# Retention feeding a multiplicative FFN on one core: the turns of keys and queries move from SyncE to ScalarE

## The chip, the cores and the metric

The kernel runs on one core of one Trainium2 chip. A core has five engines that run their own instruction streams in order: TensorE (PE in the profile, its weight loads PEld), VectorE (DVE), ScalarE (ACT), GpSimd (POOL) and SyncE (SP). They meet only through semaphores. The metric is device time in microseconds of one execution, the median of several. The kernel before takes 191.19 us (three runs, 191.11 to 193.03). One execution of it was profiled.

## The reference, cut to what matters

For four sequences, eight heads, 768 tokens and a head width of 64, a decaying state is built up, token by token, and read by the query. The result, as rows of 512, goes through two projections whose product passes two more matrices:

```
for t in range(S):
    state = gamma * state + einsum('bhd,bhe->bhde', k[:, :, t], v[:, :, t])
    y[:, :, t] = scale * einsum('bhd,bhde->bhe', q[:, :, t], state)
x = y.transpose(0, 2, 1, 3).reshape(B * S, H * D)      # 3072 x 512
out = ((x @ w1) * (x @ w2)) @ w3 @ w_out               # 512 -> 1024 -> 1024 -> 512
```

## The kernel before, in words

The recurrence is cut into chunks of 256 tokens, three to a sequence, twelve in all; the code calls a chunk a **step** and numbers them n = 0 to 11. All engines follow an order written out by hand: the Python order of the calls is the order on each engine, and every wait is put in by the framework from the tiles that are read and written. Each tile has a tag and a number of buffers (`bufs`), and the eight banks of PSUM are given to tags by name (S0, S1, X0, X1, K, F0, F1, F2).

For a step, q, k and v are loaded from HBM as float32 into `st` tiles (fifteen staging buffers; k and v come in two transfers each, q in one), cast to half precision in `q16`, `k16` and `v16` (v is scaled by the decay at the same time), and q and k are turned so that the head dimension lies on the partitions. The first steps turn on TensorE; from step 3 on the turn is a DMA transpose from SBUF to SBUF. The turned tiles feed `scores` (k by q, within the chunk) and `inter` (state by q); the untransposed k and v feed `kv`, whose result updates the state; `mask` and `av` give the chunk's output, `x_out` scales it into `XT`. Then eight units follow, `a_unit` and `b_unit` for u = 0 to 3: each is eight matmuls of 128x128 by 256 columns with w1 or w2. ScalarE copies the result of an a unit to SBUF (`a_evac`, the tile `pa`), and VectorE multiplies it with the result of the b unit (`b_evac`, the tile `ht`). One step later `o_unit` multiplies `ht` with w3 @ w_out, which is made once at the start, ScalarE scales it out of PSUM (`o_copy`, the tile `osb`) and SyncE stores it.

The units of a step share three banks, taken in turn: a0 in F2, b0 in F0, a1 in F1, b1 in F2, a2 in F0, b2 in F1, a3 in F2, b3 in F0. So `b_unit` 2 can start only when `a_evac` 1 has emptied F1, and `b_unit` 3 only when `a_evac` 2 has emptied F0.

The loop at the end of the kernel runs steps 3 to 11. A step from 4 on begins with `inter(n)`, then `ahead(n + 1)` (scores and kv of the next step), `av(n)`, `x_out(n)`, the two `o_unit`s of step n - 1, and the eight units of step n. TensorE runs this in order, so a late operand of `scores(n + 1)` holds everything behind it. SyncE issues every DMA of the kernel: in a step the turn of step n + 2 as one transposing transfer of keys and queries together (16 blocks of 128x128, `turn_pair`, L304), the loads of step n + 4, and the store of step n - 1, which waits for both `o_copy`s (L568). ScalarE casts the queries (`cast_queries`), GpSimd casts the keys and the values (`casts`). Step 3 has its own list, `catch_up`, spread over its units, because the prologue leaves stores and loads behind.

Of the kernel before, what the change touches and what calls it, by code (L numbers as in the profile page):

```python
# [10 lines left out]
HP = mybir.dt.float16  # L11
# [9 lines left out]
def kernel(  # L21
# [11 lines left out]
    nc = tc.nc  # L33
    B, H, S, D = q.shape
    T = 256
# [1 line left out]
    EO = 2  # L37
    NSTAGE = 15
    NS = B * PER
    PAIR = 3 + 2  # L40
    NP = H // 2
    DM = 512
    DFF = 1024
# [6 lines left out]
    att = ctx.enter_context(tc.tile_pool(name="att", bufs=2))  # L50
# [7 lines left out]
    def copy(eng, dst, src):  # L58
        {"v": nc.vector.tensor_copy, "g": nc.gpsimd.tensor_copy, "s": nc.scalar.copy}[eng](dst, src)  # L59

    def tt(eng, dst, a, b, op):
        (nc.vector if eng == "v" else nc.gpsimd).tensor_tensor(dst, a, b, op)  # L62
# [6 lines left out]
    def new_stage():  # L69
        return stage.tile([128, 1024], FP, tag="st", name="st")  # L70
# [4 lines left out]
    def load(nm, n, via=None):  # L75
        via = via or nc.sync
        b, c = divmod(n, PER)
        t = new_stage()
        src = source[nm][b, :, c * T : (c + 1) * T, :]
        if nm == "q" or n < EO:  # L80

            via.dma_start(
                t[:, :].rearrange("p (h x) -> p h x", x=2 * D), src.rearrange("h (p t) d -> p h (t d)", t=2)
            )
        else:
            for s in range(2):
                via.dma_start(  # L87
                    t[:, s * 512 : (s + 1) * 512].rearrange("p (h d) -> p h d", d=D),
                    src[:, s * 128 : (s + 1) * 128, :].rearrange("h i d -> i h d"),
                )  # L90
        tok_in[nm, n] = t
# [14 lines left out]
    w3_st, wo_st, w_st = {}, {}, {}  # L106
# [114 lines left out]


    w3h, w3p, w3t, acc = {}, {}, {}, {}
    w3_free = []

    def cast_wo(i, eng):
        copy(eng, WO[i][:, :, :].rearrange("p a n -> p (a n)"), wo_st[i][:, :])

    def cast_w3(f, eng):
        if not w3_free:  # L230
            pair = att.tile([128, 2, 2, 512], HP, tag="kq16", name="w3h", bufs=3)
            w3_free.extend(pair[:, i, :, :].rearrange("p t c -> p (t c)") for i in range(2))
        w3h[f] = w3_free.pop(0)
        copy(eng, w3h[f], w3_st[f][:, :])

    def turn_w3(f, tag):
        src, ps = w3h.pop(f), bank(tag, [128, 1024], HP)
# [22 lines left out]

    kq16 = {}
    q16, k16, v16, qT, kT, qP, am, XT, TS, KB, X = {}, {}, {}, {}, {}, {}, {}, {}, {}, {}, {}

    def cast(nm, n, eng):
        dst = {"q": q16, "k": k16}[nm]
        if n < PAIR:
            dst[n] = t = att.tile([128, 2, 512], HP, tag=nm + "16", name=nm + "16", bufs=2)
        else:  # L270
            if n not in kq16:
                kq16[n] = att.tile([128, 2, 2, 512], HP, tag="kq16", name="kq16", bufs=3)
            dst[n] = t = kq16[n][:, "kq".index(nm), :, :]
        src = tok_in.pop((nm, n))
        if nm == "q" or n < EO:
            copy(
                eng, t[:, :, :].rearrange("p t (h d) -> p h t d", d=D),
                src[:, :].rearrange("p (h t d) -> p h t d", t=2, d=D),
            )
        else:  # L280
            copy(eng, t[:, :, :].rearrange("p s c -> p (s c)"), src[:, :])

    def cast_v(n, eng):
        v16[n] = t = att.tile([128, 2, 512], HP, tag="v16", name="v16", bufs=3)
        src = tok_in.pop(("v", n))
        if n < EO:
            tt(
                eng, t[:, :, :].rearrange("p t (h d) -> p h t d", d=D),
                src[:, :].rearrange("p (h t d) -> p h t d", t=2, d=D),
                VS[:, :, :].rearrange("p t h -> p h t").unsqueeze(3).broadcast_to((128, H, 2, D)), MULT,  # L290
            )
        else:
            tt(
                eng, t[:, :, :].rearrange("p s (h d) -> p (s h) d", d=D),
                src[:, :].rearrange("p (s d) -> p s d", d=D),
                VN[:, :, :].rearrange("p s h -> p (s h)").unsqueeze(2).broadcast_to((128, 2 * H, D)), MULT,
            )

    def new_T(nm):
        return att.tile([128, 2, NP, 128], HP, tag=nm + "T", name=nm + "T", bufs=2)  # L300

    def turn_pair(n):
        t = att.tile([128, 2, 2, NP, 128], HP, tag="kqT", name="kqT", bufs=2)
        nc.sync.dma_start_transpose(  # L304
            t[:, :, :, :, :].rearrange("p x t a i -> p (x t a) i"),
            kq16[n][:, :, :, :].rearrange("p x t c -> p (x t c)"),
        )
        kT[n], qT[n] = t[:, 0, :, :, :], t[:, 1, :, :, :]

    def dma_turn(nm, n, via=None):  # L310
        src, dst = {"q": (q16, qT), "k": (k16, kT)}[nm]
        dst[n] = t = new_T(nm)
        (via or nc.sync).dma_start_transpose(
            t[:, :, :, :].rearrange("p t a i -> p (t a) i"), src[n][:, :, :].rearrange("p t c -> p (t c)")
        )
# [181 lines left out]
    def two_blocks(W, n, u, tag):  # L497
        ps = bank(tag, [128, 2, T])
        for i in range(2):
            f = 2 * u + i  # L500
            for d in range(4):
                nc.tensor.matmul(  # L502
                    ps[:, i, :], lhsT=W[d][:, f * 128 : (f + 1) * 128], rhs=XT[n][:, d, :],
                    start=(i == 0 and d == 0), stop=(i == 1 and d == 3),
                )
        return ps
# [5 lines left out]
    def b_evac(n, u, ps):  # L512
        if n not in HT:
            HT[n] = fsb.tile([128, 8, T], HP, tag="ht", name="ht", bufs=2)
        tt("v", HT[n][:, 2 * u : 2 * u + 2, :], pa.pop((n, u))[:, :, :], ps[:, :, :], MULT)
# [4 lines left out]
    def b_unit(n, u, tag):  # L520
        b_evac(n, u, two_blocks(W2, n, u, tag))
# [41 lines left out]
    def o_store(n, tb, c0=0, c1=512):  # L563
        r0 = n * T + tb * 128
        nc.sync.dma_start(out[r0 : r0 + 128, c0:c1], o_sb[n][:, tb, c0:c1])  # L565

    def o_store_all(n):
        nc.sync.dma_start(  # L568
            out[n * T : (n + 1) * T, :].rearrange("(t p) c -> p t c", t=2), o_sb[n][:, :, :]
        )  # L570
# [286 lines left out]
    LAST = 3  # L857

    def casts(n):
        if n < NS:  # L860
            cast("k", n, "g")
            cast_v(n, "g")

    def cast_queries(n):
        if n < NS:
            cast("q", n, "s")

    def turns(n):
        if n < NS:
            turn_pair(n)  # L870

    def loads(n):
        if n < NS:
            load("k", n)
            load("q", n, nc.sync)
            load("v", n, nc.sync)

    def catch_up(u):
        if u == 0:
            load("k", LAST + 3)  # L880
            turns(LAST + 2)
            o_store(2, 1)
            o_store(1, 1)
            o_store(2, 0)
            load("q", LAST + 3)
            load("v", LAST + 3)
        elif u == 1:
            load("k", LAST + 4)
        elif u == 3:
            casts(LAST + 3)  # L890

    def ahead(n):
        scores(n, ("S0", "S1"))
        kv(n, ("K", "F1"))

    def ahead_out(n):
        states(n)
        mask(n, 0)
        mask(n, 1)

    LATE = ()
    for n in range(LAST, NS):
        nxt = n + 1 < NS and n > LAST
        late = nxt and n in LATE
        if n > LAST:
            inter(n, ("X0", "X1"))
            fence(n)
            if nxt and not late:
                ahead(n + 1)
            av(n)  # L910
            x_out(n, 0)
            x_out(n, 1)
            if nxt and not late:
                ahead_out(n + 1)
            cast_queries(n + 2)
            turns(n + 2)
            if n == LAST + 1:
                load("q", n + 3)
                load("v", n + 3)
            loads(n + 4)  # L920
            casts(n + 3)
            o_unit(n - 1, 0, ("F2",))
            o_copy(n - 1, 0)
            o_unit(n - 1, 1, ("F0",))
            o_copy(n - 1, 1)
            o_store_all(n - 1)
        tags = ("F2", "F0", "X1" if late else "F1")
        for u in range(4):
            if late and u == 2:
                ahead(n + 1)  # L930
                for i in range(1, 4):
                    state(n + 1, i)
                mask(n + 1, 0)
            a_unit(n, u, tags[2 * u % 3])
            b_unit(n, u, tags[(2 * u + 1) % 3])
            if late and u == 2:
                mask(n + 1, 1)
            if late and u == 2 + 1:
                state(n + 1, 4)
                state(n + 1, 5)  # L940
            if n == LAST:
                catch_up(u)
    cuts = ((0, 320), (320, 512))
    o_unit(NS - 1, 0, ("F2",))
    o_out(NS - 1, 0)
# [32 lines left out]
```

## Time and profile before

| | us |
|---|---|
| median of three runs | 191.19 |
| the profiled execution, its own time | 192.26 |
| span of the profiled execution | 190.6 |
| TensorE busy in the span | 174.9 (92%) |
| ScalarE busy | 71.1 (37%) |
| GpSimd busy | 50.5 (26%) |
| queue of SyncE, its transfers, as a share of 16 DMA engines | 85.6% |

How to read it: the span is what the profiler saw of the program; the own time of the same execution has 1.66 us around it. Busy shares are averages over stages with different limits. A row of a timeline gives the start, the duration, the engine, the line, the operation and the tiles, and in brackets the idle time just before it and what ended it; "SPq" is the queue of SyncE, where the duration of a DMA instruction is the time that SyncE was held by issuing it, not the time of the transfer. Landing times run from the start of the issue until the data has arrived.

### The profile page before, as it was taken

Reading aid. Unit: us, or ns where it says so; the run is one execution under the profiler, and the core shown is the slowest. Engines: PE = TensorE matmul, PEld = TensorE weight load, DVE = VectorE, ACT = ScalarE, POOL = GpSimd, SP = SyncE. Lnnn points to the kernel's source line nnn. Section 1 sums busy time; section 2 is a strip of 40 time slices with the busy share of each in tenths; the row PEclk is TensorE's granted clock in tenths of the full one; section 3 lists DMA queues with packets and bytes.
Section 4 is the critical chain, followed back from the end, with each engine's and each line's share of the span. In section 5 each row is a group of like instructions: output and inputs, shape, how many; then the busy total and the mean of one; then the engine's idle time right before and its main releaser. Section 6 shows DMA issues by size and latency. Waiting matters only on the chain.

```text
span 190.6 us, 5952 instructions
## 1 busy us (share of the span) xinstructions
PE 174.9 (92%) x2592; PEld 125.2 (66%) x2592; DVE 100.6 (53%) x171; ACT 71.1 (37%) x131; POOL 50.5 (26%) x79
## 2 busy tenths in 40 slices
PE   7499998999999884899899969999999999999993
PEld 2254554788757652686785846868868688585872
DVE  2435788526866285538248427474384653744130
ACT  5634434462255202231534333343432432322322
POOL 7852237633230301020505233323033010000000
PEclk9979999999999999699999999999999999999999
DMA  5999999989998998999999999999998270030303
GB/s 218 399 407 357 321 290 381 413 210 235 234 212 185 206 246 179 223 252 241 203 219 193 291 198 243 237 246 229 216 292 215 39 185 3 0 115 0 108 6 110
DMA packets 83402, 40.75 MB, mean 214 GB/s; under 512 B 61232, under 2 KB 77872, under 8 KB 83376
## 3 DMA queue, kind: packets, MB, share of 16 engines
q1 hardware_dynamic: 83376, 40.38, 85.6%
q8 instruction: 20, 0.33, 0.8%
q14 instruction: 6, 0.05, 0.1%
HBM read 29.36 MB, written 6.29 MB: 187 GB/s over the span
## 4 chain that ended last, share of the span: by engine, by line
PE 57%; DMA 22%; SPq 6%; POOL 6%; issue 3%; DVE 2%; ACT 2%; POOLq 0%; DVEq 0%
PE psF L502 29%; PE psF L550 15%; DMA st<-in_k_dram 6%; DMA st<-in_v_dram 5%; DMA st<-in_moe_w_dram 4%; DMA st<-in_q_dram 4%; SPq L87 4%; DMA kqT<-kq 3%; PE psX L443 2%; PE psX L252 2%; PE psS L252 2%; SPq L565 1%; PE psX L468 1%; PE psS L353 1%; POOL v L62 1%
## 5 line engine op out<-in xcount | busy, mean ns | idle before, releaser
L502 PEld LDWEIGHTS <-w 128*128 128x128 f16 x640 | 63.3, 99 | 15.7 <-issue 5.8
L502 PE MATMUL psF<-xt,w 128*128 128x256 f16 x576 | 65.9, 276 | 4.0 <-ACT osb L561 4.0
L62 DVE TENSOR_TENSOR ht<-pa,psF 128x512 f16<-128x512 f32 x39 | 26.8, 687 | 42.3 <-PE psF L502 42.3
L550 PE MATMUL psF<-w3o,ht 128*128 128x512 f16 (+2 forms) x176 | 38.3, 370 | 0.0
L59 ACT COPY pa<-psF 128x512 f32<-128x512 f32 x39 | 22.7, 585 | 41.3 <-PE psF L502 36.6
L550 PEld LDWEIGHTS <-ht 128*128 128x128 f16 x200 | 18.4, 98 | 19.3
L62 POOL TENSOR_TENSOR v<-st,VN 128x1024 f16<-128x1024 f32 x8 | 15.2, 1902 | 33.3 <-DMA st<-in_v_dram 23.6
L561 ACT ACTIVATE osb<-psF 128x512 f32<-128x512 f32 (+2 forms) x22 | 12.6, 576 | 24.3 <-PE psF L550 24.3
L485 DVE TENSOR_TENSOR xt<-psX,YN 128x512 f16<-128x512 f32 x18 | 12.2, 725 | 8.8 <-PE psX L468 8.8
L532 PEld LDWEIGHTS <-w 128*128 128x128 f16 x128 | 12.1, 98 | 2.9 <-ACT w L59 1.3
L62 POOL TENSOR_TENSOR t<-s,GS 128x256 f16<-128x256 f32 x8 | 5.8, 726 | 30.5 <-DVE s L62 30.5
L252 PEld LDWEIGHTS <-w3t 128*128 128x128 f16 x64 | 5.8, 101 | 7.3 <-ACT w3t L59 1.6
L370 DVE TENSOR_TENSOR am<-psS,keep 128x512 f16<-128x512 f32 x15 | 9.6, 681 | 1.2 <-PE psX L353 1.2
L59 ACT CAST kq<-st 128x1024 f16<-128x1024 f32 x7 | 7.3, 1046 | 6.7 <-DMA st<-in_q_dram 6.7
L532 PE MATMUL psF<-xt,w 128*128 128x256 f16 x56 | 9.7, 273 | 0.0
L59 POOL CAST kq<-st 128x1024 f16<-128x1024 f32 x6 | 6.2, 1036 | 12.2 <-DMA st<-in_k_dram 12.2
L443 PEld LDWEIGHTS <-t 64*64 64x64 f16 x320 | 6.2, 109 | 3.1 <-issue 3.0
L240 PEld LDWEIGHTS <-w3h 128*128 128x128 f16 x64 | 4.4, 110 | 4.5 <-DVE w3h L59 3.5
L532 PE MATMUL psX<-xt,w 128*128 128x256 f16 x32 | 6.1, 273 | 0.8 <-ACT w L59 0.8
L502 PE MATMUL psS<-xt,w 128*128 128x256 f16 x48 | 5.7, 272 | 1.0 <-DVE ht L62 1.0
L468 PE MATMUL psX<-am,v 64*64 64x64 f16 (+1 forms) x320 | 6.0, 197 | 0.5 <-ACT fence L456 0.5
L468 PEld LDWEIGHTS <-v 64*64 64x64 f16 x384 | 5.0, 106 | 1.8 <-issue 0.9
(137 smaller groups left out, 201.3 us busy)
## 6 DMA issues: line engine op xcount, KB each, us to landing
st<-in_moe_w_dram SPq DMA_DIRECT2D x16, 512.0 KB, 8.9
st<-in_q_dram SPq DMA_DIRECT2D x12, 512.0 KB, 6.6
st<-in_v_dram SPq DMA_DIRECT2D x20, 256.0 KB, 5.9
st<-in_k_dram SPq DMA_DIRECT2D x20, 256.0 KB, 5.4
out_dram<-osb SPq DMA_DIRECT2D x8, 512.0 KB, 5.0
st<-in_moe_w_out_dram SPq DMA_DIRECT2D x4, 512.0 KB, 7.3
out_dram<-osb SPq DMA_DIRECT2D x7, 256.0 KB, 3.8
st<-in_k_dram SPq DMA_DIRECT2D x2, 512.0 KB, 10.1
```

The source lines that it names most:

```text
L59: {"v": nc.vector.tensor_copy, "g": nc.gpsimd.tensor_copy, "s": nc.scalar.copy}[eng](dst, src)
L62: (nc.vector if eng == "v" else nc.gpsimd).tensor_tensor(dst, a, b, op)
L87: via.dma_start(t[:, s * 512 : (s + 1) * 512].rearrange("p (h d) -> p h d", d=D), src[:, s * 128 : (s + 1) * 128, :].rearrange("h i d -> i ...
L252: nc.tensor.matmul(acc[f][:, :], lhsT=w3t[f][:, g * 128 : (g + 1) * 128], rhs=WO[i][:, r, :], start=(first and r == 0), stop=(last and r = ...
L370: nc.vector.tensor_tensor(t[:, :, :, :].rearrange("p a s i -> p (a s) i"), ps[:, :, :, :].rearrange("p a s i -> p (a s) i"), keep64[:, :]. ...
L443: nc.tensor.matmul(o, lhsT=TS[n, c][half(r), a, :], rhs=rhs, start=((g, r) not in begun), stop=False, skip_group_check=True,)
L468: nc.tensor.matmul(o, lhsT=v16[n][half(g), t, h * D : (h + 1) * D], rhs=rhs, start=((g, r) not in begun), stop=(n >= EO or t == 1), skip_g ...
L485: nc.vector.tensor_tensor(XT[n][:, :, :].rearrange("p a (s x) -> p (a s) x", s=2)[:, :, g * 64 : (g + 1) * 64].rearrange("p k (i t) -> p k ...
L502: nc.tensor.matmul(ps[:, i, :], lhsT=W[d][:, f * 128 : (f + 1) * 128], rhs=XT[n][:, d, :], start=(i == 0 and d == 0), stop=(i == 1 and d = ...
L532: nc.tensor.matmul(rows_ps[w, n, uh][j // 2][:, j % 2, :], lhsT=W[d][:, f * 128 : (f + 1) * 128], rhs=XT[n][:, d, :], start=(first and j % ...
L550: nc.tensor.matmul(ps[:, :], lhsT=HT[n][:, f, tb * 128 : (tb + 1) * 128], rhs=W3O[f][:, c0:c1], start=(f == 0), stop=(f == 7),)
L561: nc.scalar.activation(o_sb[n][:, tb, c0:c1], o_ps.pop((n, tb, c0, c1))[:, :], AF.Copy, scale=final_scale)
```

## The change

The one transposing transfer of a step becomes two of half the size, `kT` and then `qT`, and from step 4 of the loop on (the turns of chunk 6 and later) ScalarE issues them, on a DMA queue of its own: the keys' after the first pair of units of step n, the queries' after the second pair, for step n + 2. The turn of chunk 5 stays with SyncE, also in two transfers. The queries' cast moves from ScalarE to GpSimd, between those of keys and values, one step earlier than before (three steps ahead of use, not two). The loads of a step run three steps ahead, not four. The tiles of casts and turns have three buffers of their own for keys and for queries, and the w3 casts of the prologue have tiles of their own. In step 3 the whole catch-up list stands ahead of the units, with the turn of chunk 5 before the load of chunk 6's keys.

```
     def cast(nm, n, eng):
-        ... (from chunk 5 on k and q share one tile kq16, 3 buffers)
+        dst[n] = t = att.tile([128, 2, 512], HP, tag=nm + "16", name=nm + "16", bufs=3)
...
-    def turn_pair(n):
-        t = att.tile([128, 2, 2, NP, 128], HP, tag="kqT", name="kqT", bufs=2)
-        nc.sync.dma_start_transpose(...)
...
     def casts(n):
         if n < NS:
             cast("k", n, "g")
+            cast("q", n, "g")
             cast_v(n, "g")
-    def cast_queries(n):
-        if n < NS:
-            cast("q", n, "s")
-    def turns(n):
-        if n < NS:
-            turn_pair(n)
+    def turns(n, via=None):
+        if n < NS:
+            dma_turn("k", n, via)
+            dma_turn("q", n, via)
...
-    def catch_up(u):
-        if u == 0:
-            load("k", LAST + 3)
-            turns(LAST + 2)
-            ...
+    def catch_up():
+        turns(LAST + 2)
+        load("k", LAST + 3)
+        o_store(2, 1)
+        o_store(1, 1)
+        o_store(2, 0)
+        load("q", LAST + 3)
+        load("v", LAST + 3)
+        casts(LAST + 3)
...
+    TVIA = (0, 1)
     for n in range(LAST, NS):
...
-            cast_queries(n + 2)
-            turns(n + 2)
-            if n == LAST + 1:
-                load("q", n + 3)
-                load("v", n + 3)
-            loads(n + 4)
+            if not TVIA:
+                turns(n + 2)
+            loads(n + 3)
             casts(n + 3)
...
+        else:
+            catch_up()
...
             a_unit(n, u, tags[2 * u % 3])
             b_unit(n, u, tags[(2 * u + 1) % 3])
+            if TVIA and n > LAST and n + 2 < NS and u in TVIA:
+                dma_turn("kq"[TVIA.index(u)], n + 2, nc.scalar)
```

More of the change, by code (lines that the diff above doesn't have):

```diff
@@ L39 @@
     NS = B * PER
-    PAIR = 3 + 2
     NP = H // 2
@@ L223 @@
     w3h, w3p, w3t, acc = {}, {}, {}, {}
-    w3_free = []
     def cast_wo(i, eng):
@@ L229, in cast_w3 @@
     def cast_w3(f, eng):
[L230 to L234, printed above, removed]
+        w3h[f] = att.tile([128, 1024], HP, tag="w3h", name="w3h", bufs=5)
+        copy(eng, w3h[f][:, :], w3_st[f][:, :])
     def turn_w3(f, tag):
@@ L258, in w3_out @@
         copy(eng, W3O[f][:, :], acc.pop(f)[:, :])
-    kq16 = {}
     q16, k16, v16, qT, kT, qP, am, XT, TS, KB, X = {}, {}, {}, {}, {}, {}, {}, {}, {}, {}, {}
@@ L267, in cast @@
         dst = {"q": q16, "k": k16}[nm]
[L268 to L273, printed above, removed]
+        dst[n] = t = att.tile([128, 2, 512], HP, tag=nm + "16", name=nm + "16", bufs=3)
         src = tok_in.pop((nm, n))
@@ L299, in new_T @@
     def new_T(nm):
-        return att.tile([128, 2, NP, 128], HP, tag=nm + "T", name=nm + "T", bufs=2)
-    def turn_pair(n):
-        t = att.tile([128, 2, 2, NP, 128], HP, tag="kqT", name="kqT", bufs=2)
[L304 to L308, printed above, removed]
+        return att.tile([128, 2, NP, 128], HP, tag=nm + "T", name=nm + "T", bufs=3)
     def dma_turn(nm, n, via=None):
@@ L874, in loads @@
             load("k", n)
-            load("q", n, nc.sync)
-            load("v", n, nc.sync)
-    def catch_up(u):
-        if u == 0:
-            load("k", LAST + 3)
-            turns(LAST + 2)
[L882 to L890, printed above, removed]
+            load("q", n)
+            load("v", n)
+    def catch_up():
[7 more added lines that the diff above has]
+        casts(LAST + 3)
     def ahead(n):
@@ L940 @@
                 state(n + 1, 5)
-            if n == LAST:
-                catch_up(u)
     cuts = ((0, 320), (320, 512))
```

## The prediction

> **What bounds the kernel now.** I read the page first (TensorE busy 92%, no other engine above 53%), then the chain of work that ended last, from step 4 on. In time order, with start and duration in microseconds, its steady part reads:
>
> ```profile
> 117.34 6.99 PE psF L502 x64
> 124.33 0.56 PE psX L443 x28
> 124.95 0.26 PE psS L353 x24
> 125.76 3.56 PE psF L550 x16
> 129.32 6.99 PE psF L502 x64
> ```
>
> This is TensorE alone: eight units (64 matmuls at 0.109, so 0.874 for each half unit), `inter`, `scores`, two `o_unit`s, and 11.98 later the next units. Call the start of a step's units U. Scores begin at U+7.55 (124.89). The first unit copies of ScalarE (92.58, 104.56, 118.26, 130.23 and on to 178.14) lie 11.97 or 11.98 apart, but for one gap of 13.70. The list of what TensorE waited for from 76 on says why:
>
> ```profile
> PE psF L502 <- ACT osb L561: 4.0, 2, 3.3
> PE psS L353 <- DMA kqT<-kq: 1.7, 1, 1.7
> PE psX L468 <- ACT fence L456: 0.3, 1, 0.3
> ```
>
> (total, times, longest). The 3.3 lies before step 3, at the queries' load of step 5. The other wait on `osb` is 0.76, before step 4's units: `o_copy` stood behind the query cast, which waited for its load. The 1.7 is step 6: SyncE, which issues everything one after another, came to the turn of chunk 7 only at 106.55. From there on nothing but TensorE ends last, so anything the change adds shows in full once it outlasts its cover.
>
> **What goes.** At step 4, 0.76: the cast leaves ScalarE. At step 6 the gap of 13.70 is 1.72 over the others; the turn no longer stands behind SyncE's loads, so this goes too. Sum: 2.5 saved. Nothing takes their place from the loads: a step's loads go out right after the previous store, about U+1.2, and land by some U+11; GpSimd casts them from about the next U on (now 1.04 + 1.04 + 1.90, with 0.73 of state, 4.7 of 12), and the turn comes a step after that. Without that step of cover, late loads would cost their lateness once. In the catch-up the queries' load of chunk 6 goes out some 1.3 later (84.71 before, landed 89.9), so the cast ends near 92.3; ScalarE wants it near 94.3. `scores(5)` keeps its turn, issued at 78.35 as before.
>
> **What comes: two turns in ScalarE's stream.** An engine is held while it issues a DMA. The timeline of SyncE has the rows (start, time held), first for 8 blocks, as after the change, then for 16:
>
> ```profile
> 54.78 1.33 SPq L313 DMA_TRANSPOSE kT<-k  x1
> 61.65 4.17 SPq L313 DMA_TRANSPOSE qT<-q  x2
> 67.02 1.29 SPq L313 DMA_TRANSPOSE kT<-k  x1
> ...
> 118.35 3.19 SPq L304 DMA_TRANSPOSE kqT<-kq  x1
> ...
> 150.15 2.93 SPq L304 DMA_TRANSPOSE kqT<-kq  x1
> ```
>
> The two of the second row took 1.34 and 2.72 by the tile's list. So one turn holds its engine for x = 1.29 to 2.72. No row shows ScalarE issuing a DMA; these are its nearest, and I see no reason for less. Into what does x go? ScalarE in the same step:
>
> ```profile
> 118.26 0.58 ACT L59 COPY pa<-psF 128x512 f32<-128x512 f32 x1 [0.28 <-PE psF L502]
> 120.00 0.58 ACT L59 COPY pa<-psF 128x512 f32<-128x512 f32 x1 [1.16 <-PE psF L502]
> 121.75 0.58 ACT L59 COPY pa<-psF 128x512 f32<-128x512 f32 x1 [1.16 <-PE psF L502]
> ```
>
> The gap is 1.16, so every turn overruns it, and the next copy is late. Behind the turn stand `a_evac` 1 and 2, and for them wait the banks of `b_unit` 2 (starts U+4.37) and `b_unit` 3 (U+6.12). With 0.05 between instructions: the keys' turn starts at U+1.55, `a_evac` 1 at 1.60 + x, the queries' turn at 2.23 + x, `a_evac` 2 at 2.28 + 2x, and it ends at 2.86 + 2x. `b_unit` 3 is on time while x stays below some 1.6; `b_unit` 2 below 2.2.
>
> The second clock is the landing. The queries' turn starts at 2.23 + x and must have landed by U+7.55, since `scores(n + 2)` stands in the next step's head and TensorE is in order. From issue to landing (min, median, max) the trace has for `kT` and then `qT`:
>
> ```profile
> DMA to landing us min/median/max: 4.2/4.7/5.2
> ...
> DMA to landing us min/median/max: 3.8/4.9/5.9
> ```
>
> Before, the turn had nearly a whole step. Now, per step:
> - x = 1.31 (the two `kT` rows): the turn starts at 3.54; landing 3.8 gives 7.34, no stall; 4.9 gives 8.44, 0.9 late; 5.9 gives 1.9.
> - x = 2.03 (mean of the `qT` rows): `a_evac` 2 ends at 6.92, `b_unit` 3 is 0.85 late; landing 4.26 + 4.9 = 9.16 against 7.55 + 0.85, another 0.76. Sum 1.6.
> - x = 2.72, landing 5.9: 0.6 at `b_unit` 2, 1.65 at `b_unit` 3, 1.05 at scores. Sum 3.3.
>
> How often? Six steps issue turns, 4 to 9. Loads end with chunk 11's, sent in step 7. The windows by step show the DMA share at 1.02 to 1.09 up to 141, then 0.75 and 0.20; after, a step still has the same transfers (SyncE took 11.4 from one turn to the next, 118.35 to 129.71), and they start at U+1.2, just where the turns are. So steps 4 to 7 run beside loads. In 8 and 9 the last row above is the model: held 2.93 for 16 blocks, landed in 4.6, so 1.47 for 8 blocks and 1.47 + 1.67 = 3.1: the queries land at U+6.9, no stall.
>
> For the loaded steps I take 1.2, between 0.9 and 1.6: both rows are of 8 blocks beside loads. Four times 1.2 is 4.8, less 2.5 is **+2.3**.
>
> **A rule against the row.** The SyncE rows are of one issuer; the loads beside a turn held SyncE 1.05 and 1.07 each (median, keys and values). The Trainium skill, Perfetto Trace Analysis, section "DMA Instruction — HWDGE (DVE, Sync)", says that the descriptor generator is shared by the issuing sequencers and locked by one of them at a time, and that the wait for the lock counts in the issuing time. By it a turn on ScalarE could wait out a load of SyncE, and a queue of its own would not free it: x near 1.31 + 1.05 = 2.4, some 2.4 a loaded step, and a sum of +7. No run here shows two issuers, so the forecast goes by the rows.
>
> **The rivals.**
> 1. *The turns fit* (faster). For: two `kT` rows held 1.3, one `qT` landed in 3.8, and in a queue of its own a turn stands behind no load. Then no stall: -2.5. Against: both medians are beyond the 4.0 that is left.
> 2. *They nearly fit.* At landing 4.3 to 4.8 and x = 1.3, 0.3 to 0.8 a loaded step: 1.2 to 3.2 against 2.5, so -1.3 to +0.7.
> 3. *ScalarE is held long* (slower, beyond the forecast). The place is `b_unit` 3, the price 2(x - 1.6) a step and the late landing on top; it decides from x = 1.6 on. Against: only one of four rows is that long. At 2.72 in four steps: 4 x 3.3 - 2.5 = +10.7.
> 4. *The change doesn't do what it says*: the turns wait on ScalarE for GpSimd's casts or for an earlier turn. The built order has them behind their casts and turns of a step before, so only step 4 could be hit, with 2 to spare.
>
> **How the numbers follow.** The profiled execution took 192.26 (span 190.6 and 1.66 around it). The median of the runs, 191.19, is 1.07 under it, so on the profiled scale 194.6 is forecast, and as a median 191.19 + 2.3 = **193.5**. Chances: forecast (192.2 to 195.5) 0.35; turns fit (188.7) 0.22; nearly fit (189.9 to 191.9) 0.22; held long (195.5 to 202) 0.20, the fourth rival 0.01. The range takes in 188.7, with 0.5 for a changed catch-up below, and most of the third rival: **188.2 to 199.8**. About 1% is what a measurement of this kernel tells from no change: 189.28 to 193.10. Faster by more: the first rival and a little, 0.23. Within: the second and the lower part of the forecast, 0.25. Slower by more: 0.52.
>
> **What would show it.** In the profile after: two transposes a step as rows of ScalarE's queue, with x as their duration; the copies behind them later than 1.75 apart; TensorE waiting for `qT` at scores (step right) or not at all (rival 1), or at the units for `pa` or `ht` (rival 3); units of steps 4 to 7 some 13.2 apart and those of 8 to 10 at 12.0; no wait of 0.76 and 1.7 as now. Wrong would make me, above all, an x on ScalarE that is far from SyncE's, or turns that land in their own queue sooner than behind loads.

## The result

The kernel after takes 202.60 us (median of four runs, 200.47 to 203.91), the kernel before, beside it on the same chip, 192.11 (191.11 to 193.16). The ratio is 1.0508, with a 95% interval of 1.0385 to 1.0632: slower. The forecast was 193.5, the range 188.2 to 199.8. The sign was the likelier one; the loss, 10.5 by these medians, is more than four times the forecast 2.3, and the time lies outside the range. The ratios here and below leave out executions over 1.5% above the fastest of their kernel, so they differ a little from those of the medians; the profiled execution of the kernel after, the slowest of its four and 1.3 above their median, is one of these.

The profiled execution of the kernel after took 203.91 (span 202.2), that of the kernel before 192.26. The working below goes by these two: 11.65 more.

### The profile after

What TensorE waited for from step 3 on (total, times, longest), the view whose lines of before named `osb` and `kqT`:

```profile
PE psS L334 <- DMA qT<-q: 9.6, 5, 3.8
PE psF L483 <- DVE ht L61: 1.9, 1, 1.9
PE psF L483 <- ACT pa L58: 1.0, 1, 1.0
```

The wait of 0.76 on `osb` at step 4 is gone, and so is that of 1.7 on `kqT` at step 6. In their place `scores` (L334) waits five times for the turned queries, and once a unit waits for a copy `pa` that ScalarE made late. The 1.9 lies in step 3.

The chain of work that ended last, in order of time (start, duration), which before held nothing but TensorE:

```profile
92.48 8.20 DMA qT<-q
100.73 0.64 PE psS L334 x26
...
102.22 5.75 PE psF L531 x16
107.97 3.21 PE psF L483 x30
111.19 8.01 DMA qT<-q
119.24 0.45 PE psS L334 x32
...
141.92 6.17 DMA qT<-q
...
155.38 4.89 DMA qT<-q
...
164.85 6.99 PE psF L483 x64
```

Two things are to be seen. The transfer of the queries is a link of the chain in steps 4, 5 and 7, with 8.20, 8.01 and 6.17 us, and in step 8, when the loads are over, with 4.89. And the two `o_unit`s (L531, the program line of `o_unit` after) took 5.75 in the step that waited longest; in the chain of before they took 3.56. Nothing in the change touches `o_unit`.

The first copy of ScalarE in each step gives the length of the steps:

| from step | 4 | 5 | 6 | 7 | 8 | 9 |
|---|---|---|---|---|---|---|
| before | 11.98 | 13.70 | 11.97 | 11.98 | 11.98 | 11.98 |
| after | 18.66 | 17.49 | 13.59 | 13.61 | 12.19 | 11.97 |
| wait for `qT` | 3.81 | 2.65 | 1.47 | 1.47 | 0.17 | none |
| wait for `pa` | none | 0.98 | none | none | none | none |
| both `o_unit`s (before 3.63) | 5.82 | 5.32 | 3.63 | 3.63 | 3.63 | 3.63 |

Step 4 starts 2.36 earlier than before (first copy 90.22 against 92.58). The steps of this table add up to 87.51 after and 73.59 before, 13.92 more, less the 2.36 that is 11.56, the whole difference but for 0.09.

One slow step as ScalarE saw it, step 5 (start, time, what it was; "ACTq" is ScalarE's queue, its duration the time that the issue held the engine):

```profile
108.88 0.58 ACT L58 COPY pa<-psF 128x512 f32<-128x512 f32 x1 [0.28 <-PE psF L483]
108.94 2.07 ACTq L294 DMA_TRANSPOSE kT<-k  x1
111.11 0.58 ACT L58 COPY pa<-psF 128x512 f32<-128x512 f32 x1 [1.64 <-PE psF L483]
111.19 3.14 ACTq L294 DMA_TRANSPOSE qT<-q  x1
114.42 1.07 ACT L58 COPY pa<-psF 128x512 f32<-128x512 f32 x2 [2.73 <-PE psF L483]
```

The second turn held ScalarE for 3.14; the third copy, at 114.42, is the one that `b_unit` 3 waited 0.98 for. Here the third rival's mechanism is seen, in this step only. The turn itself landed 8.0 after its start, and TensorE, in the same profile:

```profile
119.24 0.45 PE L334 MATMUL psS<-qT,kT 64*64 64x64 f16 x32 [2.65 <-DMA qT<-q]
...
120.15 5.32 PE L531 MATMUL psF<-w3o,ht 128*128 128x512 f16 x16
...
134.54 0.45 PE L334 MATMUL psS<-qT,kT 64*64 64x64 f16 x32 [1.47 <-DMA qT<-q]
...
135.43 3.63 PE L531 MATMUL psF<-w3o,ht 128*128 128x512 f16 x16
```

After a wait of 2.65 the same sixteen matmuls took 5.32, after one of 1.47 they took 3.63. The windows around the first (stretch, length, busy time and instructions of TensorE, its weight loads, VectorE, ScalarE and GpSimd, then the granted clock, the DMA share, GB/s) say why:

```profile
117.00:119.00 2.00, 0.00 (x0) 0.10 (x1) 0.00 (x0) 0.00 (x0) 0.00 (x0) 1.00 1.34 232
119.00:121.00 2.00, 1.76 (x99) 1.24 (x99) 0.63 (x2) 0.00 (x0) 0.00 (x0) 0.82 1.22 281
121.00:123.00 2.00, 2.00 (x6) 0.65 (x5) 1.90 (x6) 0.00 (x0) 0.00 (x0) 0.50 1.16 184
123.00:125.00 2.00, 2.00 (x9) 0.89 (x8) 1.58 (x3) 0.60 (x1) 1.47 (x2) 0.83 0.00 0
```

The granted clock fell to 0.50 after the wait and came back some 3.4 us later. The prediction had no term for this.

### The profile page after: what moved, and what is told of

It reads as the page before. It is cut to its first block, busy times and chain, and to the rows that moved or that the text cites. A ratio compares the mean times of both kernels' runs of the same rounds, so it can differ in the third digit from the quotient of the medians.

```text
span 202.2 us, 5966 instructions
## 1 busy us (share of the span) xinstructions
PE 178.7 (88%) x2592; PEld 126.7 (63%) x2592; DVE 99.7 (49%) x171; ACT 65.6 (32%) x125; POOL 56.6 (28%) x85
## 4 chain that ended last, share of the span: by engine, by line
PE 42%; DMA 35%; SPq 7%; POOL 5%; DVE 3%; issue 3%; ACTq 2%; ACT 1%; POOLq 0%; DVEq 0%
DMA qT<-q 13%; PE psF L483 13%; PE psF L531 12%; DMA st<-in_v_dram 8%; DMA st<-in_k_dram 7%; SPq L86 5%; DMA st<-in_moe_w_dram 3%; DMA st<-in_q_dram 3%; PE psS L247 2%; POOL v L61 2%; ACTq L294 2%; PE psX L247 2%; PE psK L247 2%; PE psF L247 2%; DVE ht L61 2%
## 5 line engine op out<-in xcount | busy, mean ns | idle before, releaser
L483 PE MATMUL psF<-xt,w 128*128 128x256 f16 x576 | 64.7, 273 | 3.9 <-DVE ht L61 1.9
L531 PE MATMUL psF<-w3o,ht 128*128 128x512 f16 (+2 forms) x176 | 42.2, 396 | 0.0
L531 PEld LDWEIGHTS <-ht 128*128 128x128 f16 x200 | 19.5, 103 | 22.2 <-issue 4.7
L466 DVE TENSOR_TENSOR xt<-psX,YN 128x512 f16<-128x512 f32 x18 | 12.2, 723 | 17.7 <-PE psX L449 17.7
L58 POOL CAST k<-st 128x1024 f16<-128x1024 f32 x8 | 8.3, 1036 | 25.5 <-DMA st<-in_k_dram 13.7
L513 PEld LDWEIGHTS <-w 128*128 128x128 f16 x128 | 12.2, 98 | 1.8
L58 POOL CAST q<-st 128x1024 f16<-128x1024 f32 x8 | 8.3, 1038 | 14.9 <-DMA st<-in_q_dram 14.9
L334 PE MATMUL psS<-qT,kT 64*64 64x64 f16 x240 | 3.9, 201 | 9.6 <-DMA qT<-q 9.6
L334 PEld LDWEIGHTS <-kT 64*64 64x64 f16 x320 | 4.3, 111 | 9.9 <-issue 8.6
L513 PE MATMUL psF<-xt,w 128*128 128x256 f16 x56 | 9.7, 273 | 0.0
L424 PE MATMUL psX<-qT,t 64*64 64x64 f16 (+1 forms) x288 | 7.5, 195 | 0.5 <-DMA qT<-q 0.5
L247 PE MATMUL psS<-wo,w3t 128*128 128x512 f16 x16 | 5.6, 475 | 1.1 <-ACT w3t L58 1.1
## 6 DMA issues: line engine op xcount, KB each, us to landing
st<-in_k_dram SPq DMA_DIRECT2D x2, 512.0 KB, 10.2
```

Source lines behind the costliest of these rows:

```text
L247: nc.tensor.matmul(acc[f][:, :], lhsT=w3t[f][:, g * 128 : (g + 1) * 128], rhs=WO[i][:, r, :], start=(first and r == 0), stop=(last and r = ...
L334: nc.tensor.matmul(ps[r][half(g), a, s, :], lhsT=kT[n][half(r), s, a, half(g)], rhs=qchunk(n, r, a, s, g), start=True, stop=True,)
L424: nc.tensor.matmul(o, lhsT=TS[n, c][half(r), a, :], rhs=rhs, start=((g, r) not in begun), stop=False, skip_group_check=True,)
L466: nc.vector.tensor_tensor(XT[n][:, :, :].rearrange("p a (s x) -> p (a s) x", s=2)[:, :, g * 64 : (g + 1) * 64].rearrange("p k (i t) -> p k ...
L483: nc.tensor.matmul(ps[:, i, :], lhsT=W[d][:, f * 128 : (f + 1) * 128], rhs=XT[n][:, d, :], start=(i == 0 and d == 0), stop=(i == 1 and d = ...
L513: nc.tensor.matmul(rows_ps[w, n, uh][j // 2][:, j % 2, :], lhsT=W[d][:, f * 128 : (f + 1) * 128], rhs=XT[n][:, d, :], start=(first and j % ...
```

## The experiments

The theory formed on this profile: a turn that goes out in a second queue, while SyncE's loads are in flight, shares the DMA engines with them and lands late (**landing**). The rival: the harm is in ScalarE's stream, which the issue holds up (**hold**). A further theory: a long wait of TensorE costs a second time, through its clock (**clock**). The ratio is to the kernel before on the same chip.

| run | what it is | median, us | ratio, 95% interval | lengths of steps 4 to 8, us |
|---|---|---|---|---|
| e1_sp_turns | after, turns by SyncE at the head of the step | 189.96 | 0.980 (0.969 to 0.992) | 12.0, 11.9, 12.0, 12.0, 13.0 |
| e2_act_head | after, turns by ScalarE at the head | 198.46 | 1.028 (1.021 to 1.036) | 17.0, 12.2, 13.9, 13.3, 12.4 |
| e3_gate_loads | after, loads held until the turns are out | 197.26 | 1.020 (1.010 to 1.030) | 16.1, 13.0, 12.0, 12.0, 12.9 |
| e4_pair_act | before, its one turn by ScalarE | 202.44 | 1.041 (1.028 to 1.054) | 13.7, 16.9, 13.9, 13.3, 11.9 |
| e5_sp4_gate | e3, step 4's turns by SyncE | 196.33 | 1.014 (0.999 to 1.028) | 12.0, 18.3, 12.0, 12.0, 13.1 |
| e6_no_late_loads | after without the loads of chunks 8 to 11 | 192.70 (two runs) | none | 16.8, 12.2, 12.0, 12.0, 12.2 |
| e7_fill | after, TensorE kept busy in two waits | 203.61 | 1.059 (1.045 to 1.072) | 14.9, 15.8, 16.7, 13.6, 12.0 |
| e8_pool_q | before, queries cast by GpSimd | 192.90 | 1.003 (0.997 to 1.010) | 12.0, 13.0, 12.0, 12.0, 12.5 |
| e9_pair_loads3 | e8, loads three ahead | 190.06 | 0.987 (0.980 to 0.995) | 12.0, 11.9, 12.0, 12.0, 12.6 |
| e10_sp_turns_again | e1 again | 188.60 | 0.982 (0.975 to 0.989) | 12.0, 11.9, 12.0, 12.0, 12.5 |

### Who issues: e1 and e2

e1 takes from the change that ScalarE issues, and with it the place behind the units:

```
-    TVIA = (0, 1)
+    TVIA = ()        # turns(n + 2) by SyncE at the head of the step, ahead of loads(n + 3)
```

> The kernel after, but SyncE issues the two turns of step n + 2 at the head of step n, ahead of its loads; casts on GpSimd and loads three steps ahead stay. If the loss sits in the issuer and its place (late landing of a turn sent in mid-step by ScalarE, or ScalarE held by sending it), the waits for qT of 9.6 us and the two unit waits of 2.9 us go and the time is 188.7 to 191. If it sits in the loads or the casts, step spacings of 13.6 and more stay and the time is 196 or above. A third outcome, 192 to 195, would say that SyncE now waits for the casts before it may send the next loads.

From step 4 on TensorE waited nowhere for `qT`, and steps 4 to 7 are 11.9 to 12.0 long. SyncE's timeline of e1 in step 6:

```profile
113.31 1.82 SPq L294 DMA_TRANSPOSE kT<-k  x1
115.23 2.44 SPq L294 DMA_TRANSPOSE qT<-q  x1
117.72 1.20 SPq L86 DMA_DIRECT2D st<-in_k_dram  x2
```

The turns stand ahead of the loads of the step, in the same queue. Their holds, 1.82 and 2.44, are no shorter than ScalarE's in after; nobody waits behind SyncE. So the loss comes with the issuer and its place in the step, and the rest of the change is worth about 2%.

e2 issues at the same place in the order, but by ScalarE:

```
-            if not TVIA:
-                turns(n + 2)
+            if n > LAST + 1:
+                turns(n + 2, nc.scalar)      # at the head of steps 5 on; step 4 as in after
...
-            if TVIA and n > LAST and n + 2 < NS and u in TVIA:
+            if TVIA and n == LAST + 1 and u in TVIA:
```

> The kernel after, but from step 5 on ScalarE issues both turns at the head of the step (behind the fences, ahead of o_copy), with nearly a whole step to land; in step 4 they stay behind the units. Theory L (the turns land late beside the loads, and nothing else): steps 5 to 9 are 12.0 apart, what step 4 loses (some 6.7 us) stays, 193 to 195. Rival H (ScalarE is held too long by issuing): two turns of 1.4 to 3.1 us do not fit into the idle 2.4 us ahead of o_copy, so the units start 1 to 2 us late in each loaded step, 197 to 200.

The landing from issue to data (min, median, max) in steps 5 to 8, beside loads, first `kT`, then `qT`, in e1:

```profile
DMA to landing us min/median/max: 5.0/5.3/6.9
...
DMA to landing us min/median/max: 4.4/5.3/6.0
```

and in e2:

```profile
DMA to landing us min/median/max: 7.5/7.9/8.5
...
DMA to landing us min/median/max: 7.3/9.0/10.2
```

Same tiles, same place in the step: in a queue of its own beside the loads the turn lands some 2.6 to 3.7 us later, by the medians. That is the landing theory. But in e2, from step 5 on, the turns went out so early that this did no harm; what was lost there is the hold theory's. The waits of TensorE in e2, and ScalarE's rows in step 6:

```profile
PE psF L483 <- ACT osb L542: 5.7, 5, 2.3
PE psS L334 <- DMA qT<-q: 3.3, 1, 3.3
```

```profile
127.37 1.25 ACTq L294 DMA_TRANSPOSE kT<-k  x1
128.72 3.82 ACTq L294 DMA_TRANSPOSE qT<-q  x1
132.64 0.60 ACT L542 ACTIVATE osb<-psF 128x512 f32<-128x512 f32 x1 [5.18 <-issue]
```

`o_copy` stands behind 5.1 us of issuing, and the units wait for its bank. (The 2.3 lies before step 3, so 3.4 of the 5.7 is the hold's.) The 3.3 is step 4, whose turns are those of after. So both costs are real: mid-step the landing, at the head the hold. Neither place on ScalarE is free.

### Are the loads the cause: e6, e3, e5

e6 leaves out the loads of chunks 8 to 11; their casts read the tiles of chunk 7 again, so that its time is that of less transfer:

```
+        if 7 < n < NS:
+            for nm in "kqv":
+                tok_in[nm, n] = kept[nm]      # no load
...
```

> The kernel after, with the loads of chunks 8 to 11 left out (their casts read the tiles of chunk 7 again, so the later third of the output is not the reference's). Turns stay in mid-step on ScalarE. Theory L: step 4 still loses as before (the loads of chunk 7 are in flight), from step 5 on the turns land in 3.1 to 4 us and ScalarE is held 1.25 to 1.6 us by each, steps are 12.0 apart: 193 to 197. If the place on ScalarE or the second queue is slow by itself, the landing stays at 6 us or more without any load: 200 to 203.

From step 5 on, where no load runs, the landings are (first `kT`, then `qT`)

```profile
DMA to landing us min/median/max: 4.0/4.0/5.3
...
DMA to landing us min/median/max: 3.2/3.4/4.8
```

Eight of the ten turns held ScalarE 1.4 to 1.6 (the others 1.25 and 2.80), and the steps are 12.0 to 12.3 long, with ScalarE issuing as in after. Step 4, whose turns run beside the loads of chunk 7, still took 16.75 (landing of the queries 8.1). So a second queue alone is not slow: the loads beside it are the cause.

e3 keeps the loads and moves them behind the turns: SyncE first sends 64 bytes of `pa` of the third pair, then the loads of step n + 4.

```
+            if n > LAST and n + 4 < NS and u == 2:
+                gate(n, u)        # nc.sync.dma_start(t, pa[n, u][0:1, 0, 0:16])
+                loads(n + 4)
...
```

> The kernel after, but SyncE sends the loads of step n + 4 only when ScalarE has copied a unit 2 of step n (a transfer of 64 bytes from pa, which SyncE has to issue first, holds them), so that from step 5 on the turns of a step run without loads beside them. Theory L (loads beside the turns make them land late): qT lands in 3.2 to 4.0 us in steps 5 to 7 instead of 6 to 8, these steps are 12.0 to 12.5 apart, 193 to 196. Rival H (ScalarE held): no change of the issue time, 200 to 203. If the loads then come too late for the casts, waits for kT or k16 appear instead.

Steps 6 and 7 came down to 12.0, step 5 to 13.0; step 4, whose loads the gate doesn't reach, stayed at 16.1. In step 5 a turn still held ScalarE 3.63, and the copy behind it was 1.0 late. The time, 197.26, lies between the two expectations. e5 gave step 4's turns to SyncE as well:

```
-            if not TVIA:
+            if n == LAST + 1:
                 turns(n + 2)
...
-            if TVIA and n > LAST and n + 2 < NS and u in TVIA:
+            if TVIA and n > LAST + 1 and n + 2 < NS and u in TVIA:
```

> The gated kernel (loads held until a unit 2 is copied), with the two turns of step 4 also given back to SyncE at the head of that step; ScalarE still issues those of steps 5 to 9 in mid-step. Theory L (only loads beside the turns cost time): what is left of the loss, the 4 us of step 4, goes, steps 5 to 9 are 12.0 to 13.0 apart, 189 to 193. If ScalarE's being held by issuing costs by itself, steps 5 to 9 are each 1 us or more over 12.0 with waits at the units, 194 to 198.

Step 4 came down to 12.0, and step 5 rose to 18.3, with a wait of 3.62 for `qT`. There SyncE was still sending the loads of chunk 8 (103.4 to 110.0) when the turns of step 5 went out (105.1 and 107.2; landing 5.1 and 7.7), so the gate had not parted them. The loss went with the overlap. In steps 6 and 7 of e5, parted, the turns landed in 3.6 to 4.9 and the steps took 11.97 and 11.98. The first expectation, 189 to 193, was missed for this one step; 196.33 lies in the range of the second, but the loss isn't spread over steps 5 to 9, as that has it. (The profiled execution took 197.50.)

### The split doesn't matter: e4

The kernel before, with its one transfer of 16 blocks issued by ScalarE behind the first pair of units:

```
-            turns(n + 2)
...
+            if n > LAST and n + 2 < NS and u == 0:
+                turn_pair(n + 2, nc.scalar)
```

> The kernel before with one part of the change alone: ScalarE issues the turn, as one transfer of 16 blocks, behind the first pair of units; casts and loads stay as before. Theory L: it lands 8 to 12 us after its issue at U+1.5 while loads run (needed at U+7.55), so 2 to 6 us are lost in each of five loaded steps, 200 to 215. Rival H alone: ScalarE is held 3 to 4 us, b_unit 2 starts about 1.4 us late in each of six steps, 197 to 200, with waits of TensorE at the units and none at scores.

TensorE's waits (here with the lines of before):

```profile
PE psF L502 <- ACT pa L59: 5.8, 4, 2.9
PE psF L502 <- ACT osb L561: 2.9, 1, 2.9
PE psS L353 <- DMA kqT<-kq: 2.6, 3, 1.5
```

The unsplit turn is held in one piece, 1.41, 5.14 and 3.39 beside loads and still 3.61 in step 9, when they are over, and so the greater part of the loss is now in front of the units (`pa`, 5.8), the smaller at scores; it landed in 8.1, 10.9 and 8.3, against 4.6 to 7.0 from SyncE before. (The 2.9 lies before step 3, as in before.) The loss is near that of after: moving the issue alone is enough for it.

### The clock: e7

In after, twelve matmuls of zeros are put ahead of `scores` of chunks 6 and 7, where it waits, so that TensorE doesn't stand idle as long:

```
     def ahead(n):
+        if n in (6, 7):
+            warm(12, "S0")
         scores(n, ("S0", "S1"))
```

> The kernel after, with twelve matmuls on zeros (0.216 us each, 2.6 us) ahead of the scores of chunks 6 and 7, where TensorE waited 3.8 and some 2 to 3 us for the turned queries and then ran at a granted clock of 0.5 for 4 to 6 us. If the clock's fall behind the wait is part of the loss (theory C), the o_units of these two steps go from 5.8 and 5.3 us back to 3.6 and the time falls by 2 to 4 us, to 198.5 to 200.5. If the clock fell for another reason, the time stays at 202 to 204.

In both steps the clock stayed at 1.00 and the `o_unit`s took 3.63; the steps took 14.90 and 15.81, 3.8 and 1.7 less. The turns of step 4 also landed earlier here (5.4 and 6.9, in after 6.3 and 8.2), so the 3.8 isn't the clock's alone; nor is the 1.7, for in step 5 the wait of 0.98 for `pa` is gone as well. Then step 6 took 16.66, 3.1 more than in after. TensorE there:

```profile
131.72 0.45 PE L334 MATMUL psS<-qT,kT 64*64 64x64 f16 x32 [2.96 <-DMA qT<-q]
...
132.87 4.96 PE L531 MATMUL psF<-w3o,ht 128*128 128x512 f16 x16
```

The turn landed in 7.8 and not 6.3, the wait was 2.96 and not 1.47, and this brought the half clock with it, 1.33 in the `o_unit`s. Step 4 itself began 1.14 later: ahead of step 3's units stands one wait of 2.40 with the half clock behind it, where after waits 1.07 there and 1.89 among the units, without the half clock. Added up: -3.76 - 1.68 + 3.07 - 0.17 + 1.14 is -1.4, which is what this profile has (202.50 against 203.91); the medians differ by less than their spread. The expected gain was not there. That the clock's loss is a term of its own is shown by the filled steps; why the next turn then landed 1.5 later is not.

### What the rest of the change is worth: e8, e9, e10

e8 is the kernel before with only the queries' cast moved to GpSimd:

```
     def casts(n):
             cast("k", n, "g")
+            cast("q", n, "g")
...
-            cast_queries(n + 2)
```

> The kernel before with one other part of the change alone: the queries are cast by GpSimd, three steps ahead, instead of by ScalarE; the turn stays one transfer of SyncE, the loads four steps ahead. If the prediction's account of the waits of before holds, the 0.76 us before step 4 goes (o_copy no longer stands behind that cast) and the 1.7 us of step 6 stays: 0.3 to 0.6% faster than before, 190.5 to 192.5 beside 191.2 to 192.8. If the turn of SyncE was also held back by that cast, 1.7 goes too: 188.5 to 190.

No difference. The wait of 0.76 on `osb` at step 4 is gone, but step 4 starts no earlier (first copy 92.61, before 92.58): step 3 loses as much at another place, a wait of 2.12 for `ht`. And step 6 still waits:

```profile
PE psS L353 <- DMA kqT<-kq: 1.4, 2, 1.0
```

e9 adds the loads one step later, as the change has them:

```
-            if n == LAST + 1:
-                load("q", n + 3)
-                load("v", n + 3)
-            loads(n + 4)
+            loads(n + 3)
```

(and without the early load of chunk 7's keys in `catch_up`).

> The kernel before with GpSimd casting the queries and the loads three steps ahead instead of four; SyncE issues the turn, still one transfer of 16 blocks, at the head of the step. Compared with the run in which SyncE issues two transfers, only the split and the order of the catch-up differ. If it was SyncE's backlog of early loads that made the turn of chunk 7 late before, its wait at step 6 is gone here too and the time is 188 to 190.5. If it was the split, the wait of 1 to 1.7 us stays and the time is that of before, 191 to 193.

The wait for `kqT` is gone, and the step that took 13.70, and 13.00 in e8, takes 11.86. So the late turn of step 6 came from loads sent too early through SyncE, and loading three steps ahead takes it away, with the turn still one transfer on SyncE. (Of the 1.72 this shows the 1.02 that e8 still had; whether the other 0.70 went with the cast or differs from run to run is open.)

e10 is the kernel of e1 once more, beside e9:

> The kernel after with SyncE as issuer at the head of the step, the same kernel as in the first such run, timed in more rounds because that interval reached from 0.969 to 0.992. If its gain over before is the 2.5 us of waits that the prediction counted as saved, the ratio is 0.984 to 0.990; if it is chance of the first chip, the ratio is 0.995 to 1.005.

188.60, 1.8% faster than before (0.975 to 0.989), and the lowest median here. TensorE's waits there from step 3 on:

```profile
PE psF L483 <- DVE ht L61: 2.1, 1, 2.1
PE psF L483 <- ACT osb L542: 1.0, 1, 1.0
PE psX L449 <- issue: 0.5, 1, 0.5
```

No wait for a turn. In its profile (188.14, 4.1 under before's) some 1.25 of the gain lies in steps 4 to 9 and 2.95 ahead of step 4's units (first copy 89.63, before 92.58). The change without its ScalarE part beats both kernels.

## Why the prediction was wrong, step by step

**What goes.** Both named waits went, that of step 6 for the reason named, SyncE's loads (e8 against e9). The 0.76 is not seen by itself: e8 removes that wait and gains nothing. Instead step 4 started 2.36 earlier in after, since step 3's wait of 3.28 gave way to 1.07 and 1.89, and a stretch of half clock behind it went too. For the catch-up the prediction had only 0.5 at the lower end of its range. Together, 4.1 was saved in this profile, not 2.5. That the 2.36 is the change's is not shown: e1, e2, e6, e7 and e10 have the same code up to there, and their step 4 starts anywhere from 1.17 later (e1) to 2.95 earlier (e10) than that of before.

**The hold, x.** The 1.31 and 2.03 that the forecast rests on were right on average: in steps 4 to 7 the eight turns held ScalarE 1.40 to 3.14, mean 1.96, and only the 3.14 lies beyond SyncE's rows. The keys' turns took 1.69 on average, the queries', second in the queue, 2.23.

What the working had wrong here is the start. It lets a turn wait for the end of the copy ahead of it, and so puts the keys' turn at U+1.55. But in steps 5 to 7 each turn's issue began 0.06 to 0.09 after that copy had *begun* (in the rows above, 108.94 behind 108.88 and 111.19 behind 111.11). U, by the prediction's own rows, is 0.92 ahead of the first copy; the keys' turns started at U+0.98 to U+1.15 in steps 4 to 7. So `b_unit` 3, late in steps 5, 6 and 7 if the prediction's 2.86 + 2x is filled with the measured holds, was late once, 0.98 in step 5, where x was 2.07 and 3.14.

**The landing: the step that failed.** For the queries the prediction took 4.9, between 3.8 and 5.9, from turns in SyncE's own queue. In ScalarE's they landed after 8.2, 8.0, 6.3 and 6.2 in steps 4 to 7. Its deadline, U+7.55, was right. In step 4 (U is 89.30) the queries' turn went out at U+3.18 and landed at U+11.4, 3.8 late, as measured (3.81). In step 5 it went out at U+3.23 and landed at U+11.2, against 7.55 + 0.98: 2.7 (measured 2.65). Steps 6 and 7: out at U+2.8 and U+2.9, landed at U+9.1, 1.5 late each (1.47). So 6.2 to 8.2 in place of 4.9, with the measured starts, gives 3.8 + 3.7 + 1.5 + 1.5 = 10.5 where the prediction had 4.8. With the prediction's own starts, 2.23 + x (with the measured x), it would give some 14: the second error, 0.4 to 1.1 a step, hid part of the first. That steps 6 and 7 come near the upper estimate, 1.6 a step, is luck: that has half of it at `b_unit` 3, and nothing was lost there.

The argument behind it stood in the first rival: "in a queue of its own a turn stands behind no load". True of the issue, and wrong for the transfer. In SyncE's queue the loads of the step are sent after the turn; in a second queue they are in flight beside it. e1 against e2 shows this at one place in the step, e6 and e3 by taking the loads away. The Trainium skill, DMA: Bandwidth & Descriptors, section "Issuing engines are not separate DMA queues", says that transfers started by different engines run on the same 16 DMA engines and interleave, and that a second issuer saves only the time of initiating. The trace agrees with the first half, by the 2.6 to 3.7 us between e1 and e2; the page would have spoken against that argument. How the DMA engines share themselves out was not measured.

**The term that was missing.** Behind the waits of 3.81 and 2.65 TensorE ran at half clock. In the `o_unit`s alone this cost 5.82 - 3.63 = 2.19 and 5.32 - 3.63 = 1.69, with some 0.5 more in the scores and `av` of step 4. The measured waits of 10.4 (3.81 + 0.98 + 2.65 + 1.47 + 1.47), the clock's 4.4 and 0.6 of smaller things are the 15.4 by which steps 4 to 7 outlast 11.98. The prediction read the 3.28 of the kernel before as a wait and no more; the windows behind it, shown below, had the second loss in plain sight.

**Steps 8 and 9**, "no stall": 12.19 and 11.97, the turns landing in 3.5 to 4.9. Right but for 0.17.

**The rule against the row** (the Trainium skill, Perfetto Trace Analysis, section "DMA Instruction — HWDGE (DVE, Sync)": the lock of the descriptor generator) gave an estimate of +7, nearer to the result than +2.3, but not by what was seen. In e2 the keys' turn held ScalarE from 127.37 for 1.25, as short as in any run, while SyncE was issuing

```profile
127.25 3.73 SPq L86 DMA_DIRECT2D st<-in_v_dram  x2
```

(two loads, the first of 0.99). In all five turns of keys at the head of e2 the hold was 1.25 or 1.26, so a first turn doesn't wait out a load. The second turn was held 2.3 to 3.8 there; but SyncE alone in e1 also held its queries' turns up to 3.16, so that needs no second issuer. What did lengthen is SyncE's loads: 9.85 for the three loads of step 5 in after, 4.8 to 5.6 a step in e1. SyncE gave up the turns, and part of the time that this freed went into longer loads. Whether a lock or full queues do this is open.

**The fourth rival** occurred once, and small. In step 4 the queries' turn stood waiting for its cast:

```profile
91.41 1.04 POOL L58 CAST q<-st 128x1024 f16<-128x1024 f32 x1 [3.94 <-DMA st<-in_q_dram]
...
92.48 1.44 ACTq L294 DMA_TRANSPOSE qT<-q  x1
```

The copy ahead of the turn began at 91.96, so by the 0.06 to 0.09 of steps 5 to 7 it could have gone out some 0.4 earlier; the 2 that the prediction had to spare were not there. These 0.4 are part of the 3.81.

**Open**: why e7's third turn landed later; what decides whether the wait of some 2 us for `ht` in step 3 (e8, e1, e10) is there; and the 12.5 to 13.0 of the step from 8 to 9 in e1, e9 and e10, where the profile shows 0.96, 0.54 and 0.47 in which TensorE waited for nothing visible. (The 12.9, 13.1 and 12.5 of e3, e5 and e8 have a wait for the turn, 0.89, 1.10 and 0.45.)

## What to carry to other kernels

Here a transfer with a deadline landed sooner ahead of the bulk loads in the same queue (4.4 to 6.9) than in a second queue beside them (7.3 to 10.2), and in the second queue it held up whatever stood behind it on the new issuer. Before moving such a transfer away from the loads, try it ahead of them. A landing time holds only for the queue and the company that it was measured in: price a moved transfer with the loads in flight beside it, not with the old queue's rows. And where a wait of TensorE grows past some 2 us, look at the granted clock behind the waits already in the trace, and add what it costs.

## What the runs showed of the hardware

**The half clock comes in pieces of 3.4 us.** The windows of the kernel *before* around its wait of 3.28 (it ends at 77.06) are these, with the granted clock third from the right:

```profile
76.00:77.00 1.00, 0.00 (x0) 0.00 (x0) 0.00 (x0) 1.00 (x2) 0.00 (x0) 0.94 0.99 229
77.00:78.00 1.00, 0.94 (x5) 0.68 (x5) 0.44 (x1) 0.01 (x1) 0.00 (x0) 0.50 0.81 183
78.00:79.00 1.00, 1.00 (x7) 0.67 (x6) 0.85 (x2) 0.04 (x1) 0.00 (x0) 0.50 1.01 228
79.00:80.00 1.00, 1.00 (x7) 0.67 (x6) 0.51 (x1) 0.54 (x1) 0.00 (x0) 0.50 1.05 235
80.00:81.00 1.00, 1.00 (x9) 0.86 (x8) 1.00 (x2) 0.00 (x0) 0.00 (x0) 0.85 1.06 218
```

What is missing to 1.00 adds up, window by window, to 0.06 + 3 x 0.50 + 0.15 = 1.71, so 3.42 us at half clock. Behind after's 2.65 it is 3.4 again, behind its 3.81 twice that (6.8), behind e2's 3.27 once. Over all the profiles from step 3 on, each wait of 1.47 to 1.94 us (ten of them) left the clock at 1.00; each of 2.28 to 3.81 (thirteen) came with the half clock; of four between, 2.05, 2.11 and 2.12 did, 2.08 (e10) did not. e1's profile (192.75, above its median) and e10's (188.14) are of the same kernel, and one has the stretch and the other not. The Trainium skill, TensorE: Matmul & The Clock Gate, section "What's actually happening", gives a free-running window of 3.4 us of idleness before the clock is halved, and the same length of work before it returns. The length of the stretches agrees; the threshold doesn't, here some 2.1 us of waiting were enough.

Where a wait falls decides the close cases. The stretches of one run start whole multiples of 3.41 apart (in after at 99.80 and 120.28, six of them). Cut each run into pieces by this step, from step 3 on: all sixteen pieces with 2.05 us or more without a matmul are followed by the half clock, and of those with 1.68 or less only one is, behind after's 3.81, where the clock was at half already. In e10 the wait of 2.08 lies across the boundary at 79.31 (counted on from the end of the prologue's stretch, 14.46), and TensorE was busy 2.06 and 2.68 of the 3.41:

```profile
75.90:79.31 3.41, 2.06 (x19) 1.70 (x18) 2.43 (x4) 0.71 (x2) 0.00 (x0) 1.00 0.67 140
79.31:82.72 3.41, 2.68 (x25) 2.41 (x25) 1.94 (x4) 0.58 (x1) 0.00 (x0) 1.00 0.89 182
```

**A second queue beside loads.** A transpose of 8 blocks of 128x128 landed in 3.1 to 3.5 us at best, in 3.1 to 6.9 ahead of the loads in SyncE's queue (e1, steps 4 to 9), and in 6.2 to 10.2 in ScalarE's beside them (after and e2, steps 4 to 7 and 4 to 8).

**Two issuers gained little.** In step 5 of after ScalarE and SyncE together issued two turns and three loads from 108.94 to 119.00, 10.1 us; in e1 SyncE alone took 9.9 for the same from 113.31. In steps 6 and 7 of after it was 7.9. The time that SyncE was held by a step's three loads rose to 9.85 and 7.6 there.
